# Loading raw feed-forward weights 7 and 10 through the residual rows' buffers, and wo in four transfers, in a fused attention and feed-forward kernel

## The chip, the core and the metric

The kernel runs on one core of one Trainium2 chip. Its time is the device time of one launch in microseconds (us), from the first to the last instruction with what lies around them. TensorE (PE) does the matrix products, VectorE (DVE), ScalarE (ACT) and GpSimd (POOL) work beside it, and SyncE (SP) and ScalarE issue the transfers between the core's memory and DRAM. All data are float32; to keep the precision, each operand of a product is split into a high and a low part, and each product is made of three passes.

## The reference, cut to what matters

```python
# x: 2048 rows of 512; 32 heads of 16; window of 8 keys, 2 rows apart; F = 1792
xn = layernorm(x)
q, k, v = split(xn @ wqkv)                      # [32 heads, 2048, 16] each
logits  = q . k[pos - 2*w] / 4, w = 0..7        # masked where pos - 2*w < 0
s = (softmax(logits) @ v[pos - 2*w]) @ wo
h = relu(xn @ w1 + b1) ** 2
out = x + s * silu(h @ w2 + b2)
```

## The kernel before

**Stages.** The rows are cut into four chunks of 512 (`NCH`), eight units of 256 (`NU`) for attention and sixteen tiles of 128. A first stage normalises the rows, makes q, k and v on PE and stores them to DRAM (`sq`, `sk`, `sv`), from where ACT's queue loads them back per unit in the layout of attention. A second stage (the loop over `c` and `f` at lines 967 to 1049) is the feed-forward network: for each of the 14 blocks of 128 hidden columns `up(c, f)` makes `ph` = w1 block times the chunk (12 products), ACT makes relu, square (high part `h`) and square (in place, or `hf`), and `down(pb, f, j)` adds to four accumulators `pb`. Attention itself runs on DVE beside both stages, as a stream of pieces (`attention()`) that `pump` places among the other instructions at build time by estimated clocks. Its results go to DRAM (`so`), come back as `oq` and are multiplied with `wo` in `out_product`.

**The buffers that matter here.** `ph` has two PSUM buffers (tag `h`): `up(c, f)` can start when all readers of block f - 2 are done. In chunk 0 the last reader for blocks 2 to 11 is `lowh(f)`, a subtraction on DVE. DVE, ACT and POOL work strictly in the order in which the program lists their instructions.

**Weights.** In chunk 0 the weights of block f are made ready by `next_w()` after `up(0, f - 3)`: ACT rounds the raw halves `w1r` and `w2r` to the high parts, POOL subtracts for the low parts. The raw halves (256 KB each) come through `piece()`, four buffers with tag `z`, so two blocks are on their way at a time; `load_w(f + 2)` is recorded behind the split of block f, and its transfers wait until POOL has finished that split. wo (1 MB) goes into two raw tiles `rwo0` and `rwo1`, four transfers each (lines 984 to 986), and is split to `wot` at f = 6 to 9. The residual rows `xr` (two buffers of 256 KB, `load_r`, line 952) are first loaded at f = 9 and 10 of chunk 0.

**The order of transfers.** Only transfers sent by `queue()` are held in program order; those sent by `dma` are placed by the build. Every transfer is given one of eight landing counters in turn (`DMAHW0` to `DMAHW7` in the rows further below), over both queues, and waits at its place until the transfer that had this counter before has landed. ACT's transfers (`load_u`: q, k, v of a unit; `load_xT`) are issued from ACT's own instruction list, so what they wait for is waited for by all that ACT has behind them. The tiles of pool `p2` (`xr`, `wot`, `rwo`) take the memory of the first stage's pools, so the first transfer into it waits until the last stores of the first stage have landed and its last products are done.

Of the kernel before, what the change touches and what calls it, by code (L numbers as in the profile page):

```python
# [9 lines left out]
F32 = mybir.dt.float32  # L10
# [5 lines left out]
P = 128  # L16
S = 2048
D = 512
F = 1792
KT = D // P  # L20
NF = F // P
# [20 lines left out]
HOME = {0: 10, 1: K0, 2: T1, 3: T2, 4: T3, 5: Q0, 6: Q1, 7: K1, 8: T4, 9: V0, 10: V1}  # L42

SEVEN = range(4, 16, 2)
VSEVEN = range(6, 14, 2)

WARM = 18
# [12 lines left out]
def body(ctx: ExitStack, tc: tile.TileContext, x, wqkv, wo, w1, b1, w2, b2, out):  # L60
# [39 lines left out]
    dma = nc.sync.dma_start  # L100

    def queue(out, in_):

        tc.keep_in_program_order(dma(out, in_))
# [16 lines left out]
    def psT(name):  # L121
        return psum.tile([P, 512], F32, name=name, tag="tp", bufs=2)

    def piece(name):
        return keep.tile([P, 512], F32, name=name, tag="z", bufs=4)
# [7 lines left out]
    def split(hi, lo, src, eng):  # L133
        high(hi, lo, src)
        low(hi, lo, src, eng)
# [20 lines left out]
    def buffer(name, i):  # L156
        return wts.tile([P, 2, 2, 512], FR, name=name, tag=f"b{i}")
# [227 lines left out]
    def pump(margin=-SLACK):  # L385

        limit = clock["PE"] + margin
        flush(clock["PE"])
        while True:
            if coming[0] is None:  # L390
                coming[0] = next(stream, None)
            if coming[0] is None or clock["V"] + coming[0] > limit:
                break
            coming[0] = next(stream, None)
        if coming[0] is None:
            not_before(limit)
# [2 lines left out]
    w12 = {}  # L399

    def load_w(f):
        r1, r2 = (piece(f"{n}{f}") for n in ("w1r", "w2r"))
        send = queue if f < 2 else dma
        send(r1.rearrange("p (k c) -> p k c", c=P), w1[:, f * P:(f + 1) * P].rearrange("(k p) c -> p k c", p=P))
        send(r2, w2[f * P:(f + 1) * P, :])
        raws[f] = r1, r2

    def next_w():

        f = len(w12)  # L410
        if f < NF:
            w12[f] = buffer(f"w{f}", HOME[f]) if f in HOME else p2.tile([P, 2, 2, 512], FR, name=f"w{f}")
            for i, r in enumerate(raws.pop(f)):
                split(w12[f][:, 0, i], w12[f][:, 1, i], r, G)
            if f + 2 < NF:
                load_w(f + 2)


    NT = S // P
# [182 lines left out]
    def up(c, f):  # L602
        ph = psH(f"ph{c}_{f}")
        n = 0
        for kt in range(KT):
            for a, b in PASSES:
                PE.matmul(ph.rearrange("p (j n) -> p j n", n=P), w12[f][:, a, 0, kt * P:(kt + 1) * P],
                          xT[c][:, kt, :, b, :], start=n == 0, stop=n == 11)
                n += 1
        if f == NF - 1 and c + 1 < NCH:  # L610
            load_xT(c + 1)
        h = hpool.tile([P, 2, 512], FR, name=f"h{c}_{f}", tag="h", bufs=4)
        A.activation(ph, ph, AF.Relu, bias=b1t[:, f:f + 1])
        A.activation(h[:, 0], ph, AF.Square)

        pool = c or f < 2 or f > 11
        full = hpool.tile([P, 512], F32, name=f"hf{c}_{f}", tag="hf") if pool else ph
        A.activation(full, ph, AF.Square)
        if pool:
            G.tensor_sub(h[:, 1], full, h[:, 0].bitcast(F32))  # L620
        hs[f] = h, None if pool else ph, clock["PE"] + 2000
# [114 lines left out]
    for a in range(2, NT, 2):  # L736
        n, t = {2: 2, 4: 1}.get(a, 0), a + 2
        seven = t in SEVEN
        for i in (t, t + 1):
# [55 lines left out]
    def pair_of_seven(a):  # L795

        b, last = a + 1, a + 2 == NT
        seven = a in VSEVEN
        for s in (1, 2, 0):
# [80 lines left out]
    for a in range(2, NT, 2):  # L880
        if a >= TPC:
            for t in (a, a + 1):
                queue(sx[t // TPC][:, :, t % TPC], xts[t].bitcast(F32))
        (pair_of_seven if a in SEVEN else pair)(a)
        if a == NT - 4:
# [6 lines left out]

    p2 = ctx.enter_context(tc.tile_pool(name="p2", bufs=1))
    pws, gs, pbs = {}, {}, {}

    def begin(c, j):

        pbs[c, j] = psA(f"pb{c}_{j}")
        A.activation(pbs[c, j], b2t, AF.Copy)
# [52 lines left out]
    def load_r(t):  # L952
        xrs[t] = p2.tile([P, D], F32, name=f"xr{t}", tag="xr", bufs=2)
        dma(xrs[t], tile_rows(x, t))
# [10 lines left out]
    rwo = {}  # L965

    for c in range(NCH):
        last = c == NCH - 1
        if c == 0:
            for j in range(TPC):  # L970
                begin(c, j)
        pb = [pbs[c, j] for j in range(TPC)]
        t0 = c * TPC
        room = ROOM if c else ROOM0
        for f in range(2, NF):
            up(c, f)
            if c == 0:
                next_w()
            pump()
            if c == 0 and f in (3, 6):  # L980

                i = f // 6
                rwo[i] = p2.tile([P, 2, D], F32, name=f"rwo{i}", tag="oT", bufs=2)
                for q in range(4):
                    rows = wo[q * P + 64 * i:q * P + 64 * i + 64, :].rearrange("(g p) n -> p g n", g=2)
                    dma(rwo[i][32 * q:32 * q + 32], rows)
            if c == 0:
                if 6 <= f < 10:
                    split(wot[:, 0, f - 6], wot[:, 1, f - 6], rwo[(f - 6) // 2][:, (f - 6) % 2], G)
            elif f == 2:  # L990
                finish(t0 - 4, G)
            elif f == 3:
                finish(t0 - 3, G)
                load_r(t0 - 2)
                load_r(t0 - 1)
                trans_o(t0 - 2, psT(f"pT{t0 - 2}"))
                trans_o(t0 - 1, psT(f"pT{t0 - 1}"))
            elif f == 4:
                lowo(t0 - 2)
                lowo(t0 - 1)  # L1000
            elif f == 5:
                out_product(t0 - 2, psT(f"pw{t0 - 2}"))
            elif f == 6:
                finish(t0 - 2, G)
                out_product(t0 - 1, psT(f"pw{t0 - 1}"))
            elif f == 7:
                finish(t0 - 1, G)
            if f == 2 and c:
                load_o(c * 2 - 1, True)
            elif f >= 7:  # L1010
                load_o(c * 2, f >= 9)
            if f in (9, 10) and not last:
                load_r(t0 + f - 9)
            if f == 10:
                for i in range(2):
                    trans_o(t0 + i, psT(f"pT{t0 + i}"))
            if f == 11:
                for i in range(2):
                    lowo(t0 + i)
            if f == 11 or (last and f > 11):  # L1020
                load_o(c * 2 + 1, f > 12)
            downs = [f - 2]
            if last and f == NF - 1:
                downs = []
            elif not last and f > NF - 3:
                downs = [f - 3, f - 2] if f == NF - 1 else []
            for i in downs:
                for j in range(TPC):
                    down(pb, i, j)
            pump(room)  # L1030
            lowh(f)
        out_product(t0, psT(f"pw{t0}"))
        if last:
            out_product(t0 + 1, psT(f"pw{t0 + 1}"))
        pump(room)
        if not last:
            for j in range(TPC):
                for i in range(2):
                    down(pb, NF - 2 + i, j)
                pump(room if j < 2 else -SLACK)  # L1040
                gate(c, j, pb)
                begin(c + 1, j)
            for i in range(2):
                up(c + 1, i)
                pump(ROOM)
                lowh(i)
                load_o(c * 2 + 1, False)
            out_product(t0 + 1, psT(f"pw{t0 + 1}"))
            pump(ROOM)
        else:  # L1050
            for i in range(2, TPC):
                trans_o(t0 + i, psH(f"pT{t0 + i}"))
            for i in range(2, TPC):
                lowo(t0 + i)
            xl = xTa.tile([P, TPC, 512], F32, name="xlast", tag="xT")
            dma(xl.rearrange("p (h e) n -> p h (e n)", e=2),
                x[t0 * P:(t0 + TPC) * P, :].rearrange("(h p e) n -> p h (e n)", p=P, e=2))
            for j in range(TPC):
                for f in range(NF - 3, NF):
                    down(pb, f, j)  # L1060
                gate(c, j, pb)
                if j < 2:
                    finish(t0 + j, V, xl[:, j])
            for j in range(2, TPC):
                n = D // 2 if j == TPC - 1 else D
                for i in range(0, D, n):
                    cols = slice(i, i + n)
                    out_product(t0 + j, (psT if i else psH)(f"pw{t0 + j}_{i}"), cols)
                    finish(t0 + j, V, xl[:, j], cols)
# [21 lines left out]
```

## Time and profile before

| | |
|---|---|
| median of 3 runs | 485.3 us (485.28, 485.30, 487.21) |
| the profiled execution | 485.13 us, span 483.1 us |
| granted TensorE clock | 1.000 |
| PE busy | 477.4 us, 99% of the span |
| DVE / ACT / POOL busy | 423.0 / 240.0 / 225.3 us |
| moved by transfers | 81.47 MB, 169 GB/s on average |

The span is from the first to the last instruction. A busy engine is one that runs an instruction; for PE the ends are modelled. The lists of waits say who was idle for whom; idle time of an engine that nobody waits for costs nothing. Rows of a timeline hold the start and the duration in us, the engine, the line, the operation, what it writes and reads, and in brackets the idle time before it. Line numbers of most instructions are those of a helper (L91), so tiles tell them apart.

### The profile page before, as it was taken

The page shows a single profiled execution, that of the slowest core. Times are in us where ns is not written, and L with a number is a line of the kernel's source. Part 1 is how long each engine was busy: PE and PEld are TensorE (multiplying, and loading weights), DVE is VectorE, ACT ScalarE, POOL GpSimd, SP SyncE. Part 2 cuts the span into 40 slices and gives each one's busy share as a digit, 9 for nine tenths or more (in the row PEclk, how much of TensorE's full clock was granted, in tenths as well). Part 3 has the DMA queues.
Part 4 walks back from the last instruction along what each step waited for, and adds up shares of the span by engine and source line. Part 5 has one row for each costly group of instructions (what it writes and reads, how often), then busy time and mean ns, then how long its engine had stood idle before and what let it go on. Part 6 is the DMA issues. An engine that isn't in the chain of part 4 may idle for free.

```text
span 483.1 us, 6128 instructions
## 1 busy us (share of the span) xinstructions
PE 477.4 (99%) x2190; PEld 396.6 (82%) x2190; DVE 423.0 (88%) x352; ACT 240.0 (50%) x441; POOL 225.3 (47%) x178
## 2 busy tenths in 40 slices
PE   8999999999999999999999999999999999999996
PEld 5888888888888888888888888888888888888885
DVE  5978999899499899999999999999999999889133
ACT  5548798856566565273513345342234543423240
POOL 1459853116986699436543322434433345253210
PEclk9999999999999999999999999999999999999999
DMA  7899999998779996571627548071707725220321
GB/s 283 243 251 258 277 243 302 263 306 269 209 198 228 255 224 151 178 166 43 170 72 185 115 164 190 26 189 43 197 16 196 224 48 145 43 86 27 87 105 71
DMA packets 71002, 81.47 MB, mean 169 GB/s; under 512 B 6204, under 2 KB 55612, under 8 KB 70972
## 3 DMA queue, kind: packets, MB, share of 16 engines
q1 hardware_dynamic: 65788, 54.87, 41.3%
q10 hardware_dynamic: 5184, 26.22, 21.8%
q8 instruction: 17, 0.28, 0.2%
q14 instruction: 13, 0.11, 0.1%
HBM read 50.60 MB, written 27.32 MB: 161 GB/s over the span
## 4 chain that ended last, share of the span: by engine, by line
PE 98%; DMA 1%; DVE 0%; POOL 0%; issue 0%; ACT 0%; POOLq 0%
PE ph L91 32%; PE pb L91 32%; PE pm L91 12%; PE pq L91 9%; PE pw L91 9%; PE pv L91 4%; DMA x<-in_A_x 1%; PE pxT L91 0%; DVE z L91 0%; DVE st L91 0%; POOL rs L91 0%; DVE xn L91 0%; ACT xT0f L91 0%; DVE mv L91 0%; DVE rs L91 0%
## 5 line engine op out<-in xcount | busy, mean ns | idle before, releaser
L91 PE MATMUL pb<-w,h 128*128 128x512 f32 x672 | 160.1, 389 | 0.0
L91 PEld LDWEIGHTS pb<-w,h 128*128 128x128 f32 x672 | 126.1, 188 | 26.2
L91 POOL TENSOR_TENSOR h<-hf,h 128x512 fp32r<-128x512 f32 x46 | 67.7, 1473 | 157.5 <-ACT hf L91 157.5
L91 PE MATMUL ph<-xU,w 128*128 128x512 f32 x504 | 120.2, 389 | 0.0
L91 ACT ACTIVATE ph<-ph,b1t 128x512 f32<-128x512 f32 x56 | 37.0, 661 | 153.9 <-PE ph L91 144.0
L91 PEld LDWEIGHTS ph<-xU,w 128*128 128x128 f32 x504 | 94.6, 188 | 19.6
L91 DVE TENSOR_TENSOR pr<-k,q 128x2048 f32<-128x2048 f32 x32 | 78.7, 2460 | 3.2 <-DMA q<-sq 2.5
L91 DVE TENSOR_TENSOR pv<-v,L 128x2048 f32<-128x2048 f32 x32 | 77.3, 2417 | 3.8 <-POOL L L91 3.1
L91 DVE TENSOR_REDUCE L<-pr 128x128 f32<-128x2048 f32 x32 | 73.0, 2281 | 0.7
L91 DVE TENSOR_REDUCE v<-pv 128x256 f32<-128x2048 f32 x32 | 72.9, 2279 | 0.7
L91 PE MATMUL pw<-wot,oT 128*128 128x512 f32 (+1 forms) x204 | 45.9, 376 | 0.0
L91 PEld LDWEIGHTS pw<-wot,oT 128*128 128x128 f32 x204 | 36.8, 188 | 7.1
L91 POOL TENSOR_TENSOR w<-w1r,w 128x512 fp32r<-128x512 f32 x14 | 31.6, 2259 | 23.4 <-ACT w L91 23.2
L91 PE MATMUL ph<-xT,w 128*128 128x512 f32 x168 | 40.0, 389 | 0.0
L91 PEld LDWEIGHTS ph<-xT,w 128*128 128x128 f32 x168 | 31.5, 188 | 6.6
L91 PE MATMUL pm<-wq,S 128*128 128x512 f32 x144 | 36.8, 392 | 0.0
L91 ACT ACTIVATE h<-ph 128x512 fp32r<-128x512 f32 x56 | 33.5, 599 | 1.8
L91 PE MATMUL pq<-wq,xT 128*128 128x512 f32 x132 | 30.9, 393 | 0.0
L91 PEld LDWEIGHTS pm<-wq,S 128*128 128x128 f32 x144 | 26.2, 188 | 5.3 <-DVE S L91 0.4
L91 PEld LDWEIGHTS pq<-wq,xT 128*128 128x128 f32 x132 | 24.5, 188 | 5.9 <-ACT xT L91 0.7
L91 ACT ACTIVATE hf<-ph 128x512 f32<-128x512 f32 x46 | 27.4, 595 | 1.9 <-POOL h L91 1.9
L91 PE MATMUL pm<-wq,xt 128*128 128x512 f32 x108 | 27.6, 392 | 0.0
(96 smaller groups left out, 531.0 us busy)
## 6 DMA issues: line engine op xcount, KB each, us to landing
k<-sk ACTq DMA_DIRECT2D x8, 960.0 KB, 7.1
v<-sv ACTq DMA_DIRECT2D x8, 960.0 KB, 7.4
sx<-xt SPq DMA_DIRECT2D x12, 512.0 KB, 5.8
xU<-sx ACTq DMA_DIRECT2D x12, 512.0 KB, 5.9
x<-in_A_x SPq DMA_DIRECT2D x16, 256.0 KB, 6.4
sk<-stg SPq DMA_DIRECT2D x8, 512.0 KB, 4.3
sq<-stg SPq DMA_DIRECT2D x8, 512.0 KB, 7.5
sv<-stg SPq DMA_DIRECT2D x8, 512.0 KB, 5.0
```

What stands on the lines that cost most here:

```text
L91: return tc.keep_in_program_order(f(*a, **k))
```

## The change

Blocks 7 and 10 get their raw weights in the two `xr` buffers instead of two of the four `z` buffers. Block 7's transfers are recorded once, where pool `p2` is made; from block 5 on, the split of block f is followed by the load of block f + 3 (block 8 behind 5, 9 behind 6, 10 behind 7, 11 behind 8, 12 behind 9), none behind 10, and 13 behind 11. wo comes in four transfers of 128 rows by 512 instead of eight of 32 rows by 2 by 512; the access pattern of such a transfer in DRAM is 4 groups, 128 rows of wo apart, of 32 rows of 512 numbers.

```diff
+SPARE = 7, 10
...
     def load_w(f):
-        r1, r2 = (piece(f"{n}{f}") for n in ("w1r", "w2r"))
+        spare = f in SPARE
+        r1, r2 = (p2.tile([P, 512], F32, name=f"{n}{f}", tag="xr", bufs=2) if spare else piece(f"{n}{f}")
+                  for n in ("w1r", "w2r"))
...
-            if f + 2 < NF:
-                load_w(f + 2)
+            after = f + (2 if f < SPARE[0] - 2 or f > 10 else 3)
+            if after < NF and f != 10:
+                load_w(after)
...
     p2 = ctx.enter_context(tc.tile_pool(name="p2", bufs=1))
     pws, gs, pbs = {}, {}, {}
+    load_w(SPARE[0])
...
                 rwo[i] = p2.tile([P, 2, D], F32, name=f"rwo{i}", tag="oT", bufs=2)
-                for q in range(4):
-                    rows = wo[q * P + 64 * i:q * P + 64 * i + 64, :].rearrange("(g p) n -> p g n", g=2)
-                    dma(rwo[i][32 * q:32 * q + 32], rows)
+                for g in range(2):
+                    row = wo[64 * i + 32 * g:64 * i + 32 * g + 1, :]
+                    dma(rwo[i][:, g], bass.AP(tensor=row.tensor, offset=row.offset, ap=[[P * D, 4], [D, 32], [1, D]]))
```

The order of instructions on PE, DVE, ACT and POOL stays the same; what moves is SP's order, and the counters that transfers wait for. On SP, around the start of the second stage, stood this before (`w1r7` is block 7's first raw half, `stg14_0` the last q rows of the first stage, `v0` the attention output of unit 0):

```order
L104 DMA sq_148<-stg14_0_1393 128x8x128 [waits Activation_49]
L404 DMA w1r7_1598<-in_B_w1 128x4x128 [waits DMAHW4_49,Pool_49]
L405 DMA w2r7_1599<-in_B_w2 128x512 [waits DMAHW5_49,Pool_49]
L986 DMA rwo0_1649<-in_A_wo 32x2x512 [waits DMAHW6_49,DMAHW7_49,DMAHW2_49,PE_49]
L986 DMA rwo0_1649<-in_A_wo 32x2x512 x2
L404 DMA w1r8_1641<-in_B_w1 128x4x128 [waits DMAHW1_49,DMAHW0_49,Pool_49]
L405 DMA w2r8_1642<-in_B_w2 128x512 [waits Pool_49]
L986 DMA rwo0_1649<-in_A_wo 32x2x512 [waits DMAHW3_49]
L986 DMA rwo1_1788<-in_A_wo 32x2x512 [waits DMAHW5_49]
L339 DMA so_151<-v0_976 16x8x1024 [waits DMAHW6_49,DVE_49]
L404 DMA w1r9_1692<-in_B_w1 128x4x128 [waits DMAHW7_49,Pool_49]
L405 DMA w2r9_1693<-in_B_w2 128x512 [waits DMAHW4_49,DMAHW0_49,Pool_49]
```

and now stands this, in the same place of SP's list:

```order
L105 DMA sq_148<-stg14_0_1393 128x8x128 [waits Activation_49]
L407 DMA w1r8_1602<-in_B_w1 128x4x128 [waits DMAHW4_49,Pool_49]
L407 DMA w1r7_1567<-in_B_w1 128x4x128 [waits DMAHW6_49,DMAHW7_49,DMAHW2_49,PE_49]
L408 DMA w2r7_1568<-in_B_w2 128x512 [waits DMAHW5_49]
L408 DMA w2r8_1603<-in_B_w2 128x512 [waits Pool_49]
L991 DMA rwo0_1653<-in_A_wo 128x1x512
L991 DMA rwo0_1653<-in_A_wo 128x1x512 [waits DMAHW0_49]
L991 DMA rwo1_1790<-in_A_wo 128x1x512 [waits DMAHW1_49]
L407 DMA w1r9_1645<-in_B_w1 128x4x128 [waits DMAHW3_49,Pool_49]
L408 DMA w2r9_1646<-in_B_w2 128x512 [waits DMAHW4_49,Pool_49]
L991 DMA rwo1_1790<-in_A_wo 128x1x512 [waits DMAHW5_49]
L340 DMA so_151<-v0_976 16x8x1024 [waits DMAHW7_49,DVE_49]
```

The wait on the first stage's last stores (sk, sv, sq of `stg14`) and last product has moved from the first piece of wo to block 7's first half; block 8 has moved ahead of block 7's halves, and three of the four pieces of wo ahead of block 9. The store of `v0` waits for the counter of the first piece of `rwo0` now (`DMAHW7`), before it was that of the second (`DMAHW6`).

On ACT, around the loads of unit 2's k and q and of unit 1's v, stood this before:

```order
L91 DMA k2_1645<-sk_149 128x1x1920 [waits DMAHW7_49,DVE_49]
L91 DMA q2_1647<-sq_148 128x1x1024 [waits DMAHW4_49]
L91 ACTIVATE ph0_4_1670<-ph0_4_1670,b1t_146 128x512 [waits DVE_49,PE_49]
L91 ACTIVATE w7_1687<-w1r7_1598 128x512 [waits DMAHW3_49]
L91 ACTIVATE w8_1731<-w1r8_1641 128x512 [waits DMAHW1_49]
L91 ACTIVATE w8_1731<-w2r8_1642 128x512 [waits DMAHW2_49]
L91 DMA v1_1740<-sv_150 128x1x1920 [waits DMAHW6_49,DMAHW3_49,DVE_49]
L91 ACTIVATE ph0_6_1762<-ph0_6_1762,b1t_146 128x512 [waits DVE_49,PE_49]
```

and now (the rows in between, which are the same in both, are left out):

```order
L92 DMA k2_1649<-sk_149 128x1x1920 [waits DMAHW7_49,DMAHW2_49,DVE_49]
L92 DMA q2_1651<-sq_148 128x1x1024 [waits DMAHW6_49]
L92 ACTIVATE ph0_4_1672<-ph0_4_1672,b1t_146 128x512 [waits DVE_49,PE_49]
L92 ACTIVATE w7_1689<-w1r7_1567 128x512 [waits DMAHW7_49,DMAHW4_49]
L92 ACTIVATE w8_1733<-w1r8_1602 128x512 [waits DMAHW3_49]
L92 ACTIVATE w8_1733<-w2r8_1603 128x512
L92 DMA v1_1742<-sv_150 128x1x1920 [waits DMAHW7_49,DMAHW5_49,DVE_49]
L92 ACTIVATE ph0_6_1764<-ph0_6_1764,b1t_146 128x512 [waits DVE_49,PE_49]
```

The counters of these waits belong, by their turn, to other transfers than before. `q2` waited for the landing of `w2r7` (`DMAHW4`) and waits for that of `w2r8` now (`DMAHW6`). `k2` waits in addition for the store of the last q rows (`DMAHW2`). `v1` waits for the store of `v0` in both (`DMAHW6`, now `DMAHW7`), and besides for a piece of wo (the last of `rwo0`, now the last of `rwo1`).

## The prediction

> **What bounds the kernel now.** I read the page's busy times first, then the chain that ended last, then the busy times of one long stretch.
>
> ```profile
> PE 477.4 (99%) x2190; PEld 396.6 (82%) x2190; DVE 423.0 (88%) x352; ACT 240.0 (50%) x441; POOL 225.3 (47%) x178
> PE 98%; DMA 1%; DVE 0%; POOL 0%; issue 0%; ACT 0%; POOLq 0%
> 20.00:460.00 440.00, 439.98 (x2019) 366.97 (x2018) 400.55 (x307) 221.15 (x410) 218.62 (x157) 1.00 0.64 168
> ```
>
> PE is the bound, and between 20 and 460 us it stands still for 0.02 us in all, at the full granted clock (1.00). The change touches only 140 to 205 us. So it cannot shorten the kernel: nothing there waits that PE feels. It can only lengthen it, by making PE wait, and the question is how much room the engines behind PE have. The waits of that stretch (engine, line, releaser: us in total, times, longest) show what the change is about:
>
> ```profile
> ACT w L91 <- DMA w2r<-in_B_w: 4.4, 2, 3.7
> DVE pr L91 <- DMA q<-sq: 2.5, 1, 2.5
> ACT ph L91 <- DMA so<-v: 2.1, 1, 2.1
> ACT w L91 <- DMA w1r<-in_B_w: 2.0, 1, 2.0
> ```
>
> The room is read from two timelines. On DVE the rows `h<-ph,h` are `lowh(f)`, which frees a `ph` buffer; on PE the row `ph<-xT,w` two blocks later needs it.
>
> ```profile
> 158.43 2.29 DVE L91 TENSOR_TENSOR pr<-k,q 128x2048 f32<-128x2048 f32 x1 [2.46 <-DMA q<-sq]
> 160.64 0.68 DVE L91 TENSOR_TENSOR h<-ph,h 128x512 fp32r<-128x512 f32 x1
> 166.23 0.68 DVE L91 TENSOR_TENSOR h<-ph,h 128x512 fp32r<-128x512 f32 x1
> 183.68 0.68 DVE L91 TENSOR_TENSOR h<-ph,h 128x512 fp32r<-128x512 f32 x1
> 163.43 2.88 PE L91 MATMUL ph<-xT,w 128*128 128x512 f32 x12
> 168.87 2.88 PE L91 MATMUL ph<-xT,w 128*128 128x512 f32 x12
> 185.19 2.88 PE L91 MATMUL ph<-xT,w 128*128 128x512 f32 x12
> ```
>
> Blocks 5, 6 and 9 are freed at 161.32, 166.91 and 184.36 us; PE takes the buffers at 163.43, 168.87 and 185.19. The room shrinks from 2.1 over 2.0 to 0.8 us, since DVE works without a gap from 158.43 on and falls back on PE. So whatever delays DVE at 158.43 by more than 0.8 us reaches PE, and that start hangs on the landing of unit 2's q.
>
> **The change part by part.** *The weights.* The waits of ACT for w1r and w2r (6.4 us) should go, but PE feels none of them: worth 0. The last step of block 7's split on POOL is this row:
>
> ```profile
> 153.69 1.29 POOL L91 TENSOR_TENSOR w<-w2r,w 128x512 fp32r<-128x512 f32 x1
> ```
>
> The split of block 7 comes later by what its transfers lose, some microseconds; POOL ends it at 154.98 us now, PE needs it at 163.43, so this costs nothing unless it slips by over 8 us.
>
> *The counter that q waits for.* These rows give ACT's issues and what follows them, SP's issues, and the times from issue to landing of single transfers in short windows:
>
> ```profile
> 147.77 0.52 ACTq L91 DMA_DIRECT2D q<-sq  x1
> 161.98 0.52 ACTq L91 DMA_DIRECT2D v<-sv  x1
> 162.61 0.66 ACT L91 ACTIVATE ph<-ph,b1t 128x512 f32<-128x512 f32 x1 [2.06 <-DMA so<-v]
> 144.13 0.34 SPq L405 DMA_DIRECT2D w2r<-in_B_w  x1
> 145.68 1.41 SPq L986 DMA_DIRECT2D rwo<-in_A_wo  x3
> 155.12 0.57 SPq L339 DMA_DIRECT2D so<-v  x1
> w2r<-in_B_w SPq DMA_DIRECT2D x1, 256.0 KB, 3.6
> k<-sk ACTq DMA_DIRECT2D x1, 960.0 KB, 9.4
> rwo<-in_A_wo SPq DMA_DIRECT2D x3, 128.0 KB, 9.0
> q<-sq ACTq DMA_DIRECT2D x1, 512.0 KB, 10.6
> so<-v SPq DMA_DIRECT2D x1, 512.0 KB, 6.8
> w2r<-in_B_w SPq DMA_DIRECT2D x1, 256.0 KB, 2.8
> SPq L986 <- DMA sq<-stg: 1.1, 1, 1.1
> ```
>
> Before, q went out when w2r7 had landed (144.13 + 3.6 = 147.73; issued 147.77) and landed at 158.4. Now it waits for w2r8. Block 7's first half takes over the wait that the first piece of wo had on the last q store (1.1 us, to 145.68), so w1r7 goes out at 145.7, w2r7 at 146.1, w2r8 at 146.5. Alone, w2r8 would land in 2.8 us, at 149.3. But unit 2's k, 960 KB, starts within 0.4 us of them and took 9.4 us (to 154.8); the three small pieces of wo, issued in exactly these places, took a median of 9.0. From 145.4 to 158.4 k, those pieces and q, 1856 KB, went through: 143 KB a us, and k with three weight halves is 1728 KB, so 157.5 at the most. I take 156 for w2r8, nearest to k's landing and the pieces of wo. Then q, 512 KB: between 4.3 us (the stores of the same size in the page's list, below) and 10.6; I take 7, nearest to the 6.8 of `so<-v`: 163.0, or 4.6 us later than now. Less the room of 0.8, PE loses **3.8 us** by this alone (bounds: 156 + 4.3 gives 1.1, 157.5 + 10.6 gives 8.9).
>
> *wo in four transfers.* A transfer of 256 KB over all 16 DMA engines is cheap, as w2r shows. The question is over how many these run. The page counts packets; the list of issues counts transfers.
>
> ```profile
> DMA packets 71002, 81.47 MB, mean 169 GB/s; under 512 B 6204, under 2 KB 55612, under 8 KB 70972
> sk<-stg SPq DMA_DIRECT2D x8, 512.0 KB, 4.3
> sk<-zero SPq DMA_DIRECT2D x1, 28.0 KB
> sv<-zero SPq DMA_DIRECT2D x1, 28.0 KB
> b1t<-in_B_b SPq DMA_DIRECT2D x1, 7.0 KB, 7.6
> 324.20:325.20 1.00, 1.00 (x6) 0.84 (x5) 1.00 (x1) 0.97 (x2) 0.00 (x0) 1.00 0.06 25
> 351.20:352.20 1.00, 1.00 (x6) 0.84 (x5) 0.97 (x2) 0.86 (x2) 0.00 (x0) 1.00 0.06 23
> ```
>
> The list has 25 rows and 262 transfers, from `k<-sk` x8 to `b1t` x1. Of the 6204 packets under 512 B, 1792 are b1t's numbers (7 KB of 4 B) and 224 the two fills with zeros (14 rows of 8 x 256 B each). The other 4188 are 16 for each of 260 transfers and 14 for each of two: I read them as one closing packet per DMA engine, and the two are the fills, whose outermost count is 14. So a transfer seems to run on as many engines as its outermost count allows. wo's new pattern has 4 outermost (4 groups of 32 rows); the old had 32, all others multiples of 16. On 4 engines each carries 64 KB of a transfer. In the last two rows one engine of 16 is busy (share 0.06) and moves 23 to 25 GB/s, so one transfer takes 2.7 us there against under 1 us over 16, and what else is spread over all 16 waits for these four. [...]
>
> The sum for this: the first piece of wo starts when w2r8 is through, 156, and lands at 158.7. `so<-v` waits for just that counter and goes out then instead of 155.12. On the four engines three more pieces lie ahead of it (8.1 us), block 9's halves (32 KB an engine), q (32 KB) and its own 32 KB, 96 KB or 4.0 us at 24 GB/s: landed at 170.8. ACT's load of v waits for that landing, as it does now (161.98, 2.06 us idle for `so<-v`), and block 6's relu lies behind it: 162.61 + 8.8 = 171.4. Three passes of ACT (1.9 us) and `lowh(6)` (0.7) end at 174.0; PE wanted the buffer at 168.87: 5.1 late. From there to block 9 DVE needs 183.68 - 166.23 = 17.45 us and PE 185.19 - 168.87 = 16.32, so another 1.1 is lost: **6.2 us**. This lies over the same PE time as the 3.8 of q, so it replaces it and is not added. Bounds: 25 GB/s and w2r8 at 154.8 give 4.6; 157.5 and a third slower under load give 12.6. Nothing gives it back later, as PE has no idle time.
>
> The profiled execution took 485.13 us, the median of the runs is 485.3; 485.3 + 6.2 = **491.5**.
>
> **The rivals.**
> *wo on all 16 engines.* The fills prove little for a pattern of 4 beside 128 partitions. Then the store of v0 lands by about 165 and the q term is left: 485.3 + 3.8 = 489.1.
>
> *q behind wo on the four engines.* If q's packets on these engines wait for all of wo that was sent before, it lands not at 163 but at 156 + 10.9 + 2.7 (w9's halves and its own part) = 169.6; DVE is 11.2 late, PE 10.4: 495.7. For it speaks the first of these rows, a store sent while ACT's k and q of unit 6 were on their way; the second is the median of all its kind:
>
> ```profile
> out<-z SPq DMA_DIRECT2D x1, 256.0 KB, 7.2
> out<-z SPq DMA_DIRECT2D x15, 256.0 KB, 2.0
> ```
>
> Against it speaks that there the queue of SP waited for ACT's, not ACT's for SP's. [...]
>
> *No change to be seen.* w2r8 passes k and lands before 153, q by 159, and wo does not hold the store of v0. Then DVE's room covers it: 485.3. Everything up to a landing of q at 161.6 would still lie within 0.5% (2.4 us), about what a measurement of this kernel can tell from no change.
>
> *Faster.* Weights that come sooner end the odd stall that makes one run of three take 487.21, and DVE's products, slowed to 2.75 to 3.0 us beside POOL's splits, start sooner. It would decide if PE waited anywhere in 140 to 205 us. It does not in this execution, so the price is at most the 0.02 us above: 485.1.
>
> **How the numbers follow.** The four-engine case gets 0.50, wo on 16 engines 0.20, q behind wo 0.09, no change 0.18, faster 0.03. Faster by over 0.5% stays at 0.03; within 0.5% I put 0.19, the fourth case with a little of the first two; slower 0.78. The range reaches down into the no-change case (0.9 us of stall) and up to the q-behind-wo case: 486.2 to 496.0.
>
> **What would show it.** ACT's row `q<-sq` near 156 instead of 147.77, and DVE's first wait for q ending near 163 instead of 158.43. SP's `so<-v` near 158.7 and ACT's `v<-sv` near 171 instead of 161.98. Packets under 512 B fall by 64 if the four new transfers replace eight on 16 engines each, and by 112 if they close with 4 packets each. PE shows its first idle time in 158 to 190 us, released by DVE `h`, some 6 us in all, and none after. A PE without idle time there proves the forecast wrong; idle time released by POOL `w` proves the wrong part was the weights.

## The result, and the profile after

The kernel after takes 494.31 us (median of 6 runs, 493.59 to 495.56), the kernel before in the same comparison 486.15 us (6 runs, 485.01 to 487.79): 1.0175 times as long, with a 95% interval from 1.0154 to 1.0196. That is 8 us slower; 6.2 were forecast. The profiled execution took 494.21 us with a span of 492.4 us, 9.1 us and 9.3 us more than before.

From the page of the kernel after, the busy times, the packets and the chain that ended last; and below them the busy times of the stretch from 20 to 460 us (here for PE, PEld, DVE, ACT and POOL; the last three numbers are the granted clock, the share of the DMA engines and GB/s):

```profile
PE 480.2 (98%) x2190; PEld 396.8 (81%) x2190; DVE 427.4 (87%) x352; ACT 240.0 (49%) x441; POOL 238.9 (49%) x178
DMA packets 70890, 81.47 MB, mean 165 GB/s; under 512 B 6092, under 2 KB 55500, under 8 KB 70860
PE 78%; DMA 10%; POOL 4%; DVE 4%; issue 2%; ACT 2%; SPq 0%; ACTq 0%; POOLq 0%
20.00:460.00 440.00, 434.39 (x1978) 359.92 (x1977) 403.98 (x306) 219.33 (x407) 229.49 (x155) 1.00 0.63 166
```

PE now stands still for 5.6 us of a stretch in which it stood for 0.02. The chain that was 98% PE has 10% of transfers in it. The small packets fell from 6204 to 6092, by 112: the number that was given for wo on four engines.

Where PE stands is in its timeline, the `up` of blocks 6, 7, 8 and 13 of the first chunk; what they hang on is in the waits from 140 to 215 us (engine, line, releaser: us in total, times, longest):

```profile
159.10 3.06 PE L92 MATMUL ph<-xT,w 128*128 128x512 f32 x12 [0.87 <-DVE h L92]
167.47 4.61 PE L92 MATMUL ph<-xT,w 128*128 128x512 f32 x12 [2.59 <-DVE h L92]
175.86 3.01 PE L92 MATMUL ph<-xT,w 128*128 128x512 f32 x12 [1.06 <-DVE h L92]
202.03 3.02 PE L92 MATMUL ph<-xT,w 128*128 128x512 f32 x12 [0.86 <-DVE h L92]
```

```profile
ACT ph L92 <- DMA so<-v: 10.7, 1, 10.7
ACT ph L92 <- DMA w2r<-in_B_w: 9.0, 1, 9.0
DVE h L92 <- ACT ph L92: 7.3, 2, 4.1
DVE pr L92 <- DMA q<-sq: 3.0, 1, 3.0
ACT oT L92 <- POOL wot L92: 2.2, 1, 2.2
DVE oT L92 <- ACT oT L92: 0.4, 1, 0.4
```

All four stops are released by `lowh` on DVE. Before, blocks 6, 7 and 8 began at 157.99, 163.43 and 168.87, so PE is 1.1, 4.0 and 7.0 us late there, and 8.7 at block 13. ACT has two long waits: 9.0 us for the raw half `w2r` (its load of q sits there), which it did not have, and 10.7 us for the store of v0 (its load of v), where it had 2.1. These are the timelines of ACT, SP and DVE:

```profile
155.85 0.52 ACTq L92 DMA_DIRECT2D q<-sq  x1
156.48 0.66 ACT L92 ACTIVATE ph<-ph,b1t 128x512 f32<-128x512 f32 x1 [8.97 <-DMA w2r<-in_B_w]
172.68 0.52 ACTq L92 DMA_DIRECT2D v<-sv  x1
173.30 0.66 ACT L92 ACTIVATE ph<-ph,b1t 128x512 f32<-128x512 f32 x1 [10.73 <-DMA so<-v]
160.82 0.59 SPq L340 DMA_DIRECT2D so<-v  x1
158.35 0.69 DVE L92 TENSOR_TENSOR h<-ph,h 128x512 fp32r<-128x512 f32 x1 [4.09 <-ACT ph L92]
164.13 2.68 DVE L92 TENSOR_TENSOR pr<-k,q 128x2048 f32<-128x2048 f32 x1 [2.99 <-DMA q<-sq]
175.12 0.69 DVE L92 TENSOR_TENSOR h<-ph,h 128x512 fp32r<-128x512 f32 x1 [3.18 <-ACT ph L92]
```

Read in order: q goes out 8.1 us later than before and is there at 164.1 (before 158.4), the store of v0 lands at 172.6, and block 6's relu, behind the load of v, starts at 173.30 (before 162.61). `lowh(6)` ends at 175.81 and PE takes the buffer at 175.86. Behind the stop at block 13 stands something else, the last two rows of the waits. SP loads `oq` when the store has landed and sends the next raw weights behind that, at 174.05; so POOL splits weights and wo late. ACT's `oT`, which takes the buffer of `rwo`, waits 2.2 us for the split of wo (before 1.5), and DVE waits 0.4 us for `oT`. DVE's next product then takes 3.17 us where it took 2.42 before, for which no cause is shown, and `lowh(11)` comes after it.

How four engines make the store late is told by the semaphore events. A transfer with an outermost count that is a multiple of 16 leaves 16 events here, such as `w1r9`, q and the store; one of wo's new four leaves 5, for the first piece one at 149.95 and four from 158.16 to 159.13. The single early event comes 1.0 to 2.0 us after the issue in all four pieces; what it stands for is not shown. The four late ones I read as one for each engine. In the table, in us, each transfer with the landing of its first twelve parts and of the last four:

```
transfer      queue   issued   12 parts landed by   last 4 landed from..to
rwo0, first   SP      148.8    -                    158.2..159.1
rwo0, second  SP      149.5    -                    162.9..164.2
rwo1, first   SP      150.2    -                    166.1..167.1
w1r9          SP      150.8    157.5                167.0..167.7
w2r9          SP      154.9    161.8                167.6..168.3
q of unit 2   ACT     155.9    160.8                163.6..164.0
rwo1, second  SP      159.1    -                    170.6..171.3
store of v0   SP      160.8    164.6                171.9..172.6
```

From issue to landing the four pieces take 10.3, 14.7, 16.9 and 12.2 us; two expectations below have 17.7 for the second and 16 to 21 for all. Twelve of the sixteen parts of the store are there at 164.6. The last four wait for the pieces of wo and land 8 us later. On these four engines SP's transfers land in the order of their issue, 2.8 to 3.0 us apart for the third and fourth piece of wo and 1.3 us for the 32 KB of the store. q, in ACT's queue, takes turns with them: from 161.3 to 162.05 us 13 packets of SP's queue (2 KB each) and 12 of ACT's (4 KB) start, in six groups by turns. So q passes the third piece, sent 5.7 us before it: it is there at 164.0 and the piece at 167.1.

### The profile page after: what moved, and what is told of

It reads as the page before. It is cut to its first block, busy times and chain, and to the rows that moved or that the text cites. A ratio compares the mean times of both kernels' runs of the same rounds, so it can differ in the third digit from the quotient of the medians.

```text
span 492.4 us, 6125 instructions
## 1 busy us (share of the span) xinstructions
PE 480.2 (98%) x2190; PEld 396.8 (81%) x2190; DVE 427.4 (87%) x352; ACT 240.0 (49%) x441; POOL 238.9 (49%) x178
## 2 busy tenths in 40 slices
DMA packets 70890, 81.47 MB, mean 165 GB/s; under 512 B 6092, under 2 KB 55500, under 8 KB 70860
## 4 chain that ended last, share of the span: by engine, by line
PE 78%; DMA 10%; POOL 4%; DVE 4%; issue 2%; ACT 2%; SPq 0%; ACTq 0%; POOLq 0%
PE pb L92 25%; PE ph L92 25%; PE pm L92 11%; PE pw L92 9%; PE pv L92 4%; PE pq L92 3%; POOL w L92 2%; DMA so<-v 2%; DMA x<-in_A_x 2%; DMA w2r<-in_B_w 2%; DMA k<-sk 2%; DMA w1r<-in_B_w 1%; DVE pv L92 1%; POOL wot L92 1%; POOL L L92 1%
## 5 line engine op out<-in xcount | busy, mean ns | idle before, releaser
L92 POOL TENSOR_TENSOR h<-hf,h 128x512 fp32r<-128x512 f32 x46 | 70.5, 1534 | 123.1 <-ACT hf L92 122.4
L92 DVE TENSOR_TENSOR pr<-k,q 128x2048 f32<-128x2048 f32 x32 | 81.1, 2533 | 3.7 <-DMA q<-sq 3.0
L92 DVE TENSOR_TENSOR pv<-v,L 128x2048 f32<-128x2048 f32 x32 | 79.7, 2491 | 1.8 <-POOL L L92 1.2
L92 PE MATMUL ph<-xT,w 128*128 128x512 f32 x168 | 42.6, 405 | 5.5 <-DVE h L92 5.4
L92 POOL TENSOR_TENSOR w<-w1r,w 128x512 fp32r<-128x512 f32 x14 | 21.6, 1541 | 32.7 <-ACT w L92 23.5
L92 POOL TENSOR_TENSOR L<-L,sm_None 128x512 f32<-128x512 f32 x7 | 19.2, 2738 | 22.6 <-DVE sm_None L92 22.6
```

Of the source, the lines that this page charges most:

```text
L92: return tc.keep_in_program_order(f(*a, **k))
```

## The experiments

All ten ran beside the kernel before, whose medians in these comparisons were 485.83 to 485.97 us. The ratios are to it, with 95% intervals.

| kernel | median, us | ratio | interval |
|---|---|---|---|
| after | 494.31 | 1.0175 | 1.0154 to 1.0196 |
| weights' part alone | 488.12 | 1.0047 | 1.0028 to 1.0067 |
| wo's part alone | 495.47 | 1.0186 | 1.0158 to 1.0214 |
| after, wo over 16 engines | 488.86 | 1.0052 | 1.0028 to 1.0077 |
| wo's part alone, over 16 engines | 490.6 | 1.0089 | 1.0060 to 1.0119 |
| after, v from SP | 489.26 | 1.0082 | 1.0058 to 1.0106 |
| after, k and q from SP | 490.4 | 1.0111 | 1.0084 to 1.0137 |
| after, k, q and v from SP | 487.76 | 1.0046 | 1.0028 to 1.0064 |
| before, k and q from SP | 485.55 | 0.9992 | 0.9975 to 1.0008 |
| after, wo over 2 engines | 503.34 | 1.0347 | 1.0322 to 1.0371 |
| weights' part, k, q and v from SP | 485.24 | 0.9985 | 0.9969 to 1.0000 |

### Which part, and is it the engines?

The theory: q's counter costs some 4 us, the four engines make the rest. The rivals: the order and the counters cost, whatever the engines; or one of the two parts has it all. Four kernels share out the parts. With wo over 16 engines and all else as after:

```diff
-  dma(rwo[i][:, g], bass.AP(tensor=row.tensor, offset=row.offset, ap=[[P * D, 4], [D, 32], [1, D]]))
+  dma(rwo[i][:, g], wo[(2 * i + g) * P:(2 * i + g + 1) * P, :])
```

> The kernel after, with the same order of transfers and the same landing counters, but each of wo's four transfers takes 128 consecutive rows, so that its outermost count is 128 and not 4 (the rows of wo come in another order than the reference's). Theory: the four DMA engines are what delays the store of v0 and the counter that ACT's load of v waits for. Then the packets under 512 B lie 64 under those of before (6140), the pieces of wo land within 10 us of their issue instead of 16 to 21, the store of v0 lands by 166 instead of 172.3, ACT no longer stands 10.7 us in front of block 6's relu, and what is left is q: it still waits for w2r8 (landing near 155), lands near 161 to 162, and PE loses 2.5 to 4.5 us: 488 to 490. Rival one, order and counters count and not the engines: the time stays at 494. Rival two, q alone is harmless and all of the loss is the four engines: 486.

Measured: 488.86 us. The rows are packets, the wait of PE and DVE's first product of unit 2:

```profile
DMA packets 70938, 81.47 MB, mean 167 GB/s; under 512 B 6140, under 2 KB 55548, under 8 KB 70908
PE ph L92 <- DVE h L92: 2.4, 1, 2.4
163.88 2.88 DVE L92 TENSOR_TENSOR pr<-k,q 128x2048 f32<-128x2048 f32 x1 [1.52 <-DMA q<-sq]
ACT ph L92 <- DMA so<-v: 1.8, 1, 1.8
```

6140 is 64 below before. The store of v0 is there at 164.9 instead of 172.6, and ACT's wait in front of block 6's relu is 1.8 us instead of 10.7. With the same order and counters the kernel wins back 5.5 us of the median, so the number of engines has the larger part. q stays late (163.88), later than expected: w2r8, behind k, has fifteen of its parts there at 155.4 and the last at 157.05. Why that one lags is open; this profiled run (490.8) is the longest of the seven.

The weights' part alone (after, with the lines 984 to 986 of before for wo):

> The weights' part alone: blocks 7 and 10 through the residual rows' buffers, wo in its eight transfers of before. By the theory the weights bring nothing, but q of unit 2 still waits for a raw half (w2r7 here, sent behind unit 2's k), which lands near 155; so q lands near 161 to 162 and the time is 488 to 490, as for the kernel with wo over 16 engines. Rival one, that the weights' part is free or a gain and the loss is all wo's: 485 to 486. Rival two, that the loss is all in the weights' part: 494.

Measured: 488.12 us; in the profiled run (487.01) q is there at 161.0 and PE loses this, its `up` of blocks 7 and 11:

```profile
164.12 3.06 PE L92 MATMUL ph<-xT,w 128*128 128x512 f32 x12 [0.65 <-DVE h L92]
187.11 3.06 PE L92 MATMUL ph<-xT,w 128*128 128x512 f32 x12
```

0.7 us late at block 7, 1.9 at block 11, against 163.43 and 185.19. So neither part is harmless. q is 2.6 us late; less the room of 0.8 us at block 11 that is 1.8, near the 1.9 measured there. The first stop shows less of it, because at block 7 the room is still 2.1 us: DVE is the slower engine of these blocks (in the kernel before 17.45 us from `lowh(6)` to `lowh(9)`, where PE has 16.32 from block 8 to block 11), and what PE loses grows until block 11.

wo's part alone (before, with the new transfers):

> wo's part alone: the kernel before with wo in four transfers whose outermost count is 4. By the turn of the counters unit 2's q now waits for the second piece of wo. By the theory that piece is slow (17.7 us from issue to landing in the kernel after), so q goes out at 162 to 166 instead of 147.8, lands at 168 to 172, and PE loses 9 to 12 us: 494 to 498, as slow as both parts together or slower. Rival one, that wo's part alone costs only the store of v0: 489 to 492. Rival two, that the loss needs block 8 ahead of block 7 (the weights' part): 485 to 487.

Measured: 495.47 us, by the intervals no different from both parts together. ACT stands for the second piece of wo, and q comes 10 us late:

```profile
ACT ph L91 <- DMA rwo<-in_A_wo: 12.0, 1, 12.0
168.48 2.29 DVE L91 TENSOR_TENSOR pr<-k,q 128x2048 f32<-128x2048 f32 x1 [3.52 <-DMA q<-sq]
```

The two parts are not additive: the weights' part moves q's counter from a slow piece of wo to a raw half. The same kernel over 16 engines:

> The kernel before with wo in four transfers of 128 consecutive rows, so with the counters of the kernel with wo's part alone, but over 16 DMA engines (the rows of wo come in another order than the reference's). By the theory the second piece of wo lands with k, near 155, q lands near 160 to 162, and PE loses 0 to 4 us: 485.5 to 489; at least 5 us less than with outermost count 4. Rival, that the turn of the counters alone makes the loss: the same time as with outermost count 4, within 1 us.

Measured: 490.6 us, 4.9 us less than with four engines where the theory had at least 5, and above its 489. In the profiled run (489.2) DVE gets q at 162.56, 4.1 us late, and PE is 3.6 us late at block 11 (188.77); 4.1 less the room of 0.8 is 3.3.

### The two ways to PE, one at a time

If ACT's standing is what carries the delays to PE, loads that SP issues close these ways while the transfers stay slow. Unit 1's v from SP:

```diff
-        A.dma_start(t.rearrange("p i c -> p (i c)"), ap)
+        (nc.sync if (what, u) == ("v", 1) else A).dma_start(t.rearrange("p i c -> p (i c)"), ap)
```

> The kernel after, with unit 1's load of v issued by SP's list and not by ACT's, so that ACT has nothing to wait for in front of block 6's relu; wo still goes over four engines and unit 2's q still waits for w2r8 on ACT. Theory: of the 9.3 us by which the profiled execution of after is longer than that of before, some 3.5 come from ACT standing 10.7 us in front of that relu, and the rest from q, which lands near 164 as before. So the time falls to 489 to 491, q is still the last releaser of DVE near 164, and the second stop of PE (at block 8) is gone. Rival one, the late store of v0 delays something else than ACT (DVE's v of unit 1, the oq loads): the time stays at 493.5 to 495. Rival two, ACT's wait is all there is: 486.

Measured: 489.26 us. Waits of PE and DVE, and below them the busy times of 2 us windows after PE's stop (first number behind the length: PE; third from the right: granted clock):

```profile
PE ph L92 <- DVE h L92: 3.7, 1, 3.7
DVE pr L92 <- DMA q<-sq: 3.7, 1, 3.7
168.00:170.00 2.00, 2.00 (x6) 1.52 (x6) 1.97 (x2) 1.33 (x3) 0.90 (x1) 0.50 0.61 185
```

The store still lands at 173.5, and PE no longer stops at block 8: it has one stop, at block 7, behind q. So 0.93% of after's 1.75% (4.5 us) come from ACT standing behind v's load and not from the late data. In this profiled run, the longest of the six (491.94), 2.8 us of the 7.0 by which the span grew are PE at half clock (below).

Unit 2's k and q from SP (the condition is `(what, u) in (("k", 2), ("q", 2))`):

> The kernel after, with unit 2's k and q issued by SP's list. There the build puts q ahead of block 9 and of wo, and the counter that it waits for belongs to block 6's first half, long landed; wo goes out a few us later, still over four engines, and unit 1's v on ACT still waits for a piece of it and for the store of v0. Theory: q lands by 159 or sooner, DVE loses nothing there, and PE runs on time up to block 7; ACT still stands in front of block 6's relu until the piece of wo or the store has landed (166 to 172), which costs PE 0.5 to 6 us: 486 to 491, and PE's one stop is at block 8. Rival one, q's counter was worth little: 493.5 to 495, as after. Rival two, k and wo now collide otherwise and the split of block 9 is late: PE waits for POOL's w.

Measured: 490.4 us. Waits of ACT and PE:

```profile
ACT ph L92 <- DMA so<-v: 10.1, 1, 10.1
PE ph L92 <- DVE h L92: 1.9, 1, 1.9
```

q is there at 157.74 and PE runs to block 8 on time; then it stops once, behind ACT's wait for the store. This run takes more away than q's wait: the build now sends the store ahead of the fourth piece of wo, and it lands at 167.5 instead of 172.6. All three loads from SP:

> The kernel after, with unit 2's k and q and unit 1's v all issued by SP's list: ACT waits for no landing of wo or of a weight half through a load's counter, although wo still goes over four engines. Theory: both ways to PE are closed and the time is that of before, 485 to 486.5, with no stop of PE over 0.3 us between 150 and 190. Rival one, the slow transfers themselves (late w9, w10, late oq) cost: 488 or more, with PE or POOL waiting for transfers.

Measured: 487.76 us, 6.3 us less than after by the ratios, but 0.46% over before, which the theory did not expect. The one stop of PE over 0.3 us is at block 13:

```profile
PE ph L92 <- DVE h L92: 1.1, 1, 1.1
ACT w L92 <- DMA w1r<-in_B_w: 5.6, 1, 5.6
DVE oT L92 <- ACT oT L92: 1.1, 2, 0.9
```

Behind it stands the same as behind after's stop at block 13. SP now stands for the store in front of v and of the next raw half, which lands at 179.0; ACT waits 5.6 us for it, POOL's splits come late, and DVE waits 1.1 us for ACT's `oT`. PE is 1.2 us late from there on, of the 1.9 by which this span is longer.

The rest was put to a test of its own: the weights' part alone, with these three loads from SP and wo in its old eight transfers.

> The weights' part alone (wo in its eight transfers of before) with unit 2's k and q and unit 1's v issued by SP's list. The kernel after with these three loads on SP is still 0.5% slower than before. Theory: that rest is the slow wo transfers, which make w9, w10 and the loads behind them late; with wo on 16 engines the time is that of before within 0.3%: 485 to 487, no stop of PE over 0.3 us between 150 and 215. Rival, the rest belongs to the weights' part (other counters, other order on SP): 487.5 to 488.5 as with four engines.

Measured: 485.24 us; the stretch from 20 to 460 us is full again (PE 439.87 of 440.00):

```profile
20.00:460.00 440.00, 439.87 (x2018) 366.98 (x2017) 402.31 (x307) 221.34 (x410) 218.61 (x157) 1.00 0.64 168
```

So the rest belonged to wo's part and not to the weights'; the raw half for which ACT waited 5.6 us lands at 172.8 here, and ACT does not wait for it. No run with these three loads on SP has wo in four transfers over 16 engines, so the number of engines is not shown as the cause of this rest by itself. Does the room itself help the kernel before?

> The kernel before, with unit 2's k and q issued by SP's list, so that q goes out ahead of wo and of block 8 and its counter is long free. Theory: q lands before 156 instead of 158.1 to 158.4, DVE gains room of 1 to 2 us where it had 0.8, and the odd run of 487 to 488 of before becomes rarer: median 485.0 to 485.8, at most 0.2% faster, since PE's own work takes 483 of it. Rival, the room does not cause the spread of before's runs: the same median as before within 0.3 us.

Measured: 485.55 us, ratio 0.9992 (0.9975 to 1.0008). DVE starts on q at 157.03 without a wait for it, 1.4 us sooner, and nothing is gained that can be told from no change. Two of its twelve runs still took over 487 us, so the longer runs were not shown to become rarer. That and 485.24 are the best versions found; neither is shown to beat before.

### The suspected cost doubled

```diff
-  ap=[[P * D, 4], [D, 32], [1, D]]
+  ap=[[2 * P * D, 2], [D, 64], [1, D]]
```

> The kernel after with the suspected cost doubled: each of wo's four transfers has an outermost count of 2 (2 groups of 64 rows; the rows of wo come in another order than the reference's), all else, counters and order included, as in after. Theory: each transfer now runs on 2 engines with 128 KB on each, 5.4 us a piece instead of 2.7; packets under 512 B fall by 8 more, to 6084. On these two engines, from 156 on, lie four pieces (21.6 us), block 9's halves, q and the store of v0 (4 x 32 KB, 5.4 us): the store lands near 183 instead of 172.5, ACT stands until then, and the time rises by 9 to 13 us: 503 to 508. q takes turns with wo on these engines, so it still lands by 165. Rival one, the number of engines is not what costs: 494 as after. Rival two, q stands behind wo in these engines: q lands 5 us later than in after, and PE's first long stop is at block 7 with 7 us or more.

Measured: 503.34 us. The packets, ACT's wait for the store, PE's stop at block 8, and DVE's product with q:

```profile
DMA packets 70882, 81.47 MB, mean 162 GB/s; under 512 B 6084, under 2 KB 55492, under 8 KB 70852
181.82 0.66 ACT L92 ACTIVATE ph<-ph,b1t 128x512 f32<-128x512 f32 x1 [20.10 <-DMA so<-v]
184.38 5.40 PE L92 MATMUL ph<-xT,w 128*128 128x512 f32 x12 [13.22 <-DVE h L92]
162.44 2.29 DVE L92 TENSOR_TENSOR pr<-k,q 128x2048 f32<-128x2048 f32 x1 [2.14 <-DMA q<-sq]
```

8 packets fewer; the store lands at 181.1, with 14 of its 16 parts there at 174.4; ACT stands for 20.1 us. The time is 9.0 us over after, at the lower end of what was expected. Not all of it is the wait: PE is 15.5 us late at block 8 and 18.1 at block 9, and the 2.6 us between are PE at half clock (below). q is not later than in after, though twice as much of wo lies on each of the engines: it does not stand behind wo.

## Why the prediction was right, point by point

*No gain was possible, the weights' waits are worth nothing.* PE had no idle time to give back. With the weights' part and the three loads from SP the time is 485.24, with k and q from SP alone 485.55: the sooner weights show no gain. Block 7's split ended 6.5 us later (161.47 on POOL), under the 8 that were allowed, and PE never waits for it. But the later splits were given no cost, and they stand behind the stop at block 13.

*The counter that q waits for.* Right in its mechanism and nearly in its numbers: issue 155.85 (forecast 156), q there at 164.1 (163.0). The 7 us for q itself were 8.2, as its last four parts came 3 us behind the others, beside wo; over 16 engines they were 6.7. The case of its own, 489.1 us with wo over 16 engines, was measured as 488.86. That the times agree so well is partly luck: the kernel before took 485.97 in that comparison and not 485.3, so the loss was 2.5 us by the ratio where 3.8 were forecast. One thing was missed here. The part on the weights and q named only DVE's wait; but ACT stands at q's load too, for 9.0 us, with block 4's relu behind it. That made PE 1.1 us late at block 6, where no loss was forecast. Taking the smallest room, 0.8 us at block 11, off q's lateness was right: with the weights alone it gives 1.8 and 1.9 was measured, though the stop at block 7 was only 0.65.

*wo on four engines.* The inference from the closing packets was right: 112 fewer. The first piece landed at 159.1 (forecast 158.7). From there to the landing of the store the sum had 8.1 + 4.0 = 12.1 us; it took 13.5. This is the term that was mis-sized: the second piece, with q's part beside it, took 5.1 us where 4.0 were counted (2.7 and a third of 4.0). So the store landed at 172.6, 1.8 us later than forecast; relu started 1.9 us later (173.30 for 171.4), and PE was 7.0 us late at block 8 where 5.1 stood. Of the further 1.1 us by DVE's pace 0.5 came by block 11. Another 1.2 came by block 13, where the late splits of the weights and of wo stand in the waits, which the sum had at nothing. So the 6.2 us of the sum are 8.7 in the profiled run; the two terms that were too small outweigh the one that was too large.

*The store goes out at 158.7.* It went out at 160.82. SP was busy with the issue of block 9's half (4.23 us) and of the fourth piece (1.59 us) until then. That cost little by the landings in the table, which on the four engines follow the order of SP's issues (the fourth piece at 171.3, the store at 172.6): three pieces lay ahead either way.

*q's loss is replaced, not added.* The rows agree: block 8 starts 0.05 us after `lowh(6)`, which hangs on the store and ACT alone. The 4.0 us that PE had lost at block 7, and the 1.7 lost to the clock, lie within the 7.0. But as shares they don't separate cleanly: without v's wait 4.5 us go, without q's as well another 1.7, with wo in its old eight transfers the last 3.

*The rivals.* wo on 16 engines, q behind wo, no change and faster are all excluded by the packets, by the run with 2 engines, and by PE's stops. Of the signs given, that PE has none after 190 us was wrong (0.86 us at 202).

## What to carry to other kernels

Here the transfers of few and large pieces were the slower ones: the kernel after took 494.31 us with an outermost count of 4, 488.86 with 128 and 503.34 with 2. So look at the outermost count of a pattern, and at what is queued behind the transfer. A load that ACT issues made ACT wait here for whatever transfer had its landing counter before (9.0 us at q, 10.7 at v, and 12.0 at q with wo's part alone), and adding and moving transfers changed who waits for whom; read the new wait list of each load, and count what stands behind it on its engine. Where the engine behind was the slower one for some blocks, the room that counted was the smallest of the stretch (0.8 us at block 11) and not that at the first block (2.1): with the weights' part alone a stop of 0.65 us had become 1.9 by then.

## What was not expected of the hardware

The granted clock fell to 0.50 after some short stops of PE (of 1.9 us and more, below). These are 2 us windows of the kernel after, behind PE's stop of 2.59 us (same columns as above):

```profile
168.00:170.00 2.00, 2.00 (x6) 1.50 (x6) 1.97 (x2) 0.00 (x0) 0.00 (x0) 0.50 0.63 182
170.00:172.00 2.00, 2.00 (x8) 1.58 (x7) 1.94 (x1) 0.00 (x0) 0.00 (x0) 0.66 0.26 98
172.00:174.00 2.00, 2.00 (x11) 1.64 (x10) 0.00 (x0) 0.67 (x2) 0.00 (x0) 1.00 0.31 93
```

The clock records show half speed from 167.94 to 171.36 here, 3.41 us, which costs 1.7 us of PE's work. Behind the stop of 2.4 us (wo over 16 engines) 2 us windows have clocks of 0.90, 0.50 and 0.75, which add up to 3.4 us at half speed; behind that of 3.7 us (v from SP) 0.65, 0.50, 0.50 and 0.65, or 6.8 us. Where windows are not shown, the 12 products of `up` behind the stop, which take 2.88 us at full speed, tell of it: 4.61 us behind the stop of 1.9 us (k and q from SP, mean clock 0.995) and 5.49 behind that of 3.9 (wo's part alone, 0.993). With wo over 2 engines they took 5.40 us behind the stop of 13.2 us (mean clock 0.985), and the page has 5 tenths from 175.5 to 188.1 us, part of it still idle. Behind the stops of 0.65 to 1.4 us they took 3.01 to 3.06 us: no half clock. Four of the seven runs of after with wo over 16 engines have a mean clock of 1.000; whether PE stopped as long in them is not shown. In the kernel after the loss was hidden by the wait at block 8: the one of its six runs with a mean clock of 0.999, where the others have 0.995 or 0.996, took 494.02 us, within the range of the others (493.59 to 495.56). With v from SP it was not hidden, and that profiled run lost 2.8 us to it.
